# Operands of a last pass on VectorE, its products reordered, and loads moved in SyncE's queue

## The chip, the cores and the metric

The kernel runs on one core of a Trainium2 chip. The metric is the device time of one execution in microseconds, as the median of several runs. A separate execution is taken with the hardware profiler; all profile rows below are from that one execution.

## What is computed

An attention layer with a memory term feeds a mixture of four experts. All arrays are float32.

```python
# attention: B, H, S, D = 4, 8, 576, 64
scores = where(causal, -1e9, q @ k.T / sqrt(D))
a      = softmax(scores);  local = a @ v
q_p    = phi(q)                                  # phi(x) = (x if x > 0 else exp(x) - 1) + 1
mem    = (q_p @ M_prev) / (q_p @ z_prev + 1e-6)
x      = g * mem + (1 - g) * local               # g = sigmoid(beta), per head
x      = x.transpose(0, 2, 1, 3).reshape(2304, 512)
# experts: E, F = 4, 1024
p   = domain_probs / domain_probs.sum(-1)
out = sum over e of p[:, e] * (relu(x @ w1[e]) @ w2[e])
```

## The kernel before

Every operand of a large product is split into a high part (the value rounded to the fast matmul type, written by ScalarE or GpSimd) and a remainder (value minus high part, written by VectorE or GpSimd). A product is then three matmuls: high by high, high by remainder, remainder by high.

**Phases.** The experts are worked off in 37 phases; a phase is one half of one expert's 1024 hidden columns. In phases 0 to 28 one or two groups of 256 tokens are live. A phase has `mm1` (four blocks `fc` of hidden columns, each followed by a relu `hh` on ScalarE and a remainder `hl` on VectorE) and `mm2` (one product `y` per 128 tokens, scaled and added into `acc` by VectorE). The attention of tokens still to come is cut into steps, kept in a list that is sorted by slot and priority (`ev(slot, priority, function)`), and a planner interleaves these steps with the matmul parts by estimated costs. All attention steps are issued by phase 27.

**The last pass.** Phases 29 to 36 handle the last 768 tokens, six tiles of 128, for all experts. There `mm1` uses a scheme with seven block products in place of eight. The token matrix is cut into four blocks, and seven operands A11, S1, S2, A12, S3, S4, A22 are made of them once (`x_ops`, L946 to L978): plain blocks, or sums and differences of blocks. S3's difference is stored in the row buffer `trow`. They are made in pieces during phases 27 and 28, one piece ahead of every third matmul part. `put` (L956 to L959) writes a high part on ScalarE and a remainder on the engine it is given. The weights are turned into the corresponding seven operands by `wt_prep` (L980 to L1003), two sets per phase: four sums `tsum` (L992 to L995), three copies `wth` on ScalarE (L996 to L998), three remainders `wtl` (L999 to L1001). The sets of phase 29 are made in `mm2` of phase 28.

`tail_mm1` (L1005 to L1046) issues the seven products of a half phase, each six matmuls of 384 columns, into three PSUM banks X, Y, Z. Several products accumulate in one bank: A11, S2, S3, A22 in X, and S1, S4 in Y. What stands in a bank after a product is read by ScalarE (`keep`, into `trow`) or VectorE (`add`) before the next product may add to it. `done` makes the relu and the remainder. `tail_mm2` (L1048 on) makes the six products `yt`.

**Raw weights.** `w_dma` loads the next 256 KB block of weights into a ring `stg` of four buffers. `w_prep` (L224 to L243) turns a block into high part and remainder and then issues the load of the block four further on, which takes the buffer just used. All loads, the copies of k and q within SBUF (`dup_k` and the copies into `qz`, in `t_trk` and `t_trq`) and the output stores are issued from SyncE's one queue, in program order.

**Attention loads.** There are 28 tasks of four or five slots, each for two heads. `t_load` (L292) loads q, k and v of a task into one of two sets of buffers; it is issued seven slots ahead of the task's first slot `s0` (nine for the first task). The transposes of k come at `s0 - 4`, those of q at `s0 - 3`, the first operation on q at `s0 - 5`, the split of v at `s0`.

Of the kernel before, what the change touches and what calls it, by code (L numbers as in the profile page):

```python
# [10 lines left out]
AF = mybir.ActivationFunctionType  # L11
ALU = mybir.AluOpType
# [45 lines left out]
def tile_attention_moe(  # L58
# [13 lines left out]
    nc = tc.nc  # L72
# [127 lines left out]
        for fc in (range(HF) if i < PH0 else (0, 2, 1, 3))  # L200
    ]
    NSTG = 4
    wpos = {"dma": 0, "prep": 0}
    stg = {}

    def w_dma():
        j = wpos["dma"]
        if j >= len(wseq):
            return
        wpos["dma"] += 1  # L210
        i, kind, fc = wseq[j]
        e, hf = halves[i]
        f0 = (hf * HF + fc) * P
        t = sp.tile([P, DM], F32, tag="stg", name=f"stg{j}", bufs=NSTG)
        stg[j] = t
        if kind == "1":
            nc.sync.dma_start(
                out=t.rearrange("p (c f) -> p c f", c=NKD),
                in_=w1[e, :, f0 : f0 + P].rearrange("(c p) f -> p c f", p=P),
            )  # L220
        else:
            nc.sync.dma_start(out=t, in_=w2[e, f0 : f0 + P, :])

    def w_prep(i, kind, pool=False):  # L224
        last_ = PH0 - 3 <= i < PH0
        act = (kind == "1" or i < START[1] or last_) and not pool
        j = wpos["prep"]
        if j >= len(wseq) or wseq[j][0] != i or wseq[j][1] != kind:
            return
        wpos["prep"] += 1  # L230
        fc = wseq[j][2]
        t = stg.pop(j)
        hi, lo = (w1s if kind == "1" else w2s)[fc]
        if kind == "1":
            hi = hi.rearrange("p c f -> p (c f)")
            lo = lo.rearrange("p c f -> p (c f)")
        if act:
            nc.scalar.activation(hi, t, AF.Copy)  # L238
        else:
            nc.gpsimd.tensor_scalar(hi, t, 1.0, 1.0, ALU.mult, ALU.mult)  # L240
        dve = (last_ and fc % 2) or (i < START[1] and fc < PR["lod"])
        (nc.vector if dve else nc.gpsimd).tensor_tensor(lo, t, f(hi), ALU.subtract)  # L242
        w_dma()  # L243


    bdat = {}
# [42 lines left out]
    ]  # L289
    NSLOT = pos  # L290

    def t_load(t):  # L292
        for n, src, c0 in (("q", q, t.cs[0]), ("k", k, 0), ("v", v, 0)):
            nfull = min(t.nk, NCH - 1) - c0
            for j in range(2):
                s_ = src[t.b, 2 * t.a + j]
                nc.sync.dma_start(  # L297
                    out=t.nat[n][:, 0:nfull, j],
                    in_=s_[c0 * P : (c0 + nfull) * P].rearrange("(c p) d -> p c d", p=P),
                )  # L300
            if t.nk == NCH:
                for r in {"q": (D,), "k": (0,), "v": (0, D)}[n]:
                    nc.sync.dma_start(
                        out=t.nat[n][r : r + S - 4 * P, nfull],
                        in_=src[t.b, 2 * t.a : 2 * t.a + 2, 4 * P : S].rearrange(
                            "h p d -> p h d"
                        ),
                    )
# [411 lines left out]
    def ev(slot, prio, fn, cost=0.0):  # L720
        events.setdefault(slot, []).append((prio, len(events.get(slot, [])), fn, cost))
# [6 lines left out]
    for t in tasks:  # L728
        s0 = t.s0
        ld = s0 - 9 if t.i < 1 else s0 - 7  # L730
        PQ = PR
        if t.run not in seen:
            seen.add(t.run)
            ev(s0 - 9, 9, lambda r=t.run: batch_load(r))
            ev(s0 - 6, 9, lambda r=t.run: batch_prep(r))
        ev(ld, 8, lambda t=t: t_load(t))
        ev(s0 + PQ["phi1"][0], PQ["phi1"][1], lambda t=t: t_phi1(t))
        ev(s0 + PQ["phi2"][0], PQ["phi2"][1], lambda t=t: t_phi2(t))
        ev(s0 + PQ["phi3"][0], PQ["phi3"][1], lambda t=t: t_phi3(t))
        ev(s0 + PQ["trq"][0], PQ["trq"][1], lambda t=t: t_trq(t), 109.0 * len(t.cs))  # L740
        ev(s0 + PQ["trq"][0] + 1, 0.4, lambda t=t: run(t.lo_q))
        ev(s0 + PQ["trk"][0], PQ["trk"][1], lambda t=t: t_trk(t), 109.0 * t.nk)
        ev(s0 + PQ["trk"][0], 0.5, lambda t=t: run(t.lo_k))
        ev(s0, PQ["v"], lambda t=t: t_v(t))
        ev(s0 + PQ["trqp"][0], PQ["trqp"][1], lambda t=t: t_trqp(t), 109.0 * len(t.cs))
        ev(s0 + PQ["trqp"][0], 4.5, lambda t=t: run(t.lo_qp))
# [204 lines left out]
    def x_ops():  # L951

        X, s_ = tail["x"], tail["s"]
        s3 = tail["r"][:, 0:2]

        def put(n, src, eng):  # L956
            hi, lo = X[n]
            nc.scalar.activation(hi, src, AF.Copy)
            eng.tensor_tensor(lo, src, f(hi), ALU.subtract)  # L959

        def plain(n, i, k):
            return [lambda: put(n, a_blk(i, k), nc.gpsimd)]

        def summed(n, eng, dst, a, b, op):
            return [
                lambda: eng.tensor_tensor(dst, a, b, op),
                lambda: put(n, dst, eng),
            ]

        return (  # L970
            plain("A11", 0, 0)
            + summed("S1", nc.vector, s_, a_blk(1, 0), a_blk(1, 1), ALU.add)
            + summed("S2", nc.vector, s_, s_, a_blk(0, 0), ALU.subtract)
            + plain("A12", 0, 1)
            + summed("S3", nc.gpsimd, s3, a_blk(0, 0), a_blk(1, 0), ALU.subtract)
            + summed("S4", nc.vector, s_, a_blk(0, 1), s_, ALU.subtract)
            + plain("A22", 1, 1)
        )  # L978

    def wt_prep(i):  # L980

        j = wpos["prep"]
        if j >= len(wseq) or wseq[j][0] != i or wseq[j][1] != "1":
            return
        wpos["prep"] += 2
        t1, t2 = stg.pop(j), stg.pop(j + 1)
        hi, lo = tail["w"][wseq[j][2]]
        t = tail["t"]
        b11, b21, b12, b22 = t1[:, 0:GW], t1[:, GW:], t2[:, 0:GW], t2[:, GW:]
        t1 = t1.rearrange("p (n w) -> p n w", w=GW)  # L990
        gp = nc.gpsimd.tensor_tensor
        gp(t[:, 0], b12, b11, ALU.subtract)  # L992
        gp(t[:, 1], b22, t[:, 0], ALU.subtract)
        gp(t[:, 2], b22, b12, ALU.subtract)
        gp(t[:, 3], b21, t[:, 1], ALU.subtract)  # L995
        nc.scalar.activation(hi[:, 0:2], t1, AF.Copy)  # L996
        nc.scalar.activation(hi[:, 2], b22, AF.Copy)
        nc.scalar.activation(hi[:, 3:7], t, AF.Copy)  # L998
        gp(lo[:, 0:2], t1, f(hi[:, 0:2]), ALU.subtract)  # L999
        nc.vector.tensor_tensor(lo[:, 2], b22, f(hi[:, 2]), ALU.subtract)  # L1000
        nc.vector.tensor_tensor(lo[:, 3:7], t, f(hi[:, 3:7]), ALU.subtract)  # L1001
        w_dma()
        w_dma()  # L1003

    def tail_mm1(i, p):  # L1005
        wh, wl = tail["w"][p]
        r = tail["r"]
        bank = {}

        def product(x, n, b):  # L1010
            first = b not in bank
            if first:
                bank[b] = tail["ps"].tile([P, 512], F32, tag="tc", name=f"tc{i}_{p}{b}", bufs=5)
            ah, al = tail["x"][x]
            for c in range(2):
                cs = slice(c * P, (c + 1) * P)
                for z, (w_, x_) in enumerate(((wh, ah), (wh, al), (wl, ah))):
                    nc.tensor.matmul(  # L1018
                        bank[b][:, 0:TB],
                        lhsT=w_[:, n, cs],  # L1020
                        rhs=x_[:, c],
                        start=first and c == 0 and z == 0,
                        stop=c == 1 and z == 2,
                        skip_group_check=True,
                    )
            return bank[b][:, 0:TB]

        def keep(o, n):
            nc.scalar.activation(r[:, n], o, AF.Copy)

        def done(src, blk, fc):
            h_, l_ = tail["h"][blk][0][fc], tail["h"][blk][1][fc]
            nc.scalar.activation(h_, src, AF.Relu)
            nc.vector.scalar_tensor_tensor(l_, src, 0.0, f(h_), ALU.max, ALU.subtract)  # L1034

        def add(o, n, blk, fc):
            nc.vector.tensor_tensor(r[:, n], o, r[:, n], ALU.add)  # L1037
            done(r[:, n], blk, fc)

        keep(product("A11", 0, "X"), 0)  # L1040
        keep(product("S1", 3, "Y"), 1)
        keep(product("S2", 4, "X"), 2)
        add(product("A12", 1, "Z"), 0, 0, p)
        add(product("S3", 5, "X"), 1, 1, p + 2)
        add(product("S4", 2, "Y"), 2, 0, p + 2)
        done(product("A22", 6, "X"), 1, p)  # L1046

    def tail_mm2(i, tts):  # L1048
        e = halves[i][0]
# [384 lines left out]
```

## Time and profile before

| what | value |
|---|---|
| median of 3 runs | 1062.28 us (1061.09 to 1063.99) |
| profiled execution | 1065.9 us |
| its span, first to last instruction | 1064.0 us |
| mean granted TensorE clock | 0.982 |
| TensorE matmul busy | 1009.3 us, 95% of the span |
| VectorE, ScalarE, GpSimd busy | 720.0, 514.2, 613.0 us |
| mean DMA rate | 110 GB/s |

Busy shares are means over stages of different kinds: the main loop of phases 0 to 28 with attention in between, the two phases in which the last pass is prepared, and the last pass. PE is TensorE, DVE is VectorE, ACT is ScalarE, POOL is GpSimd, SP is SyncE; `L242` is line 242 of the kernel. A name such as `w2l<-stg,w2h` is the tile written and the tiles read.

### The profile page before, as it was taken

Reading aid. Unit: us, or ns where it says so; the run is one execution under the profiler, and the core shown is the slowest. Engines: PE = TensorE matmul, PEld = TensorE weight load, DVE = VectorE, ACT = ScalarE, POOL = GpSimd, SP = SyncE. Lnnn points to the kernel's source line nnn. Section 1 sums busy time; section 2 is a strip of 40 time slices with the busy share of each in tenths; the row PEclk is TensorE's granted clock in tenths of the full one; section 3 lists DMA queues with packets and bytes.
Section 4 is the critical chain, followed back from the end, with each engine's and each line's share of the span. In section 5 each row is a group of like instructions: output and inputs, shape, how many; then the busy total and the mean of one; then the engine's idle time right before and its main releaser. Section 6 shows DMA issues by size and latency. Waiting matters only on the chain.

```text
span 1064.0 us, 16442 instructions
## 1 busy us (share of the span) xinstructions
PE 1009.3 (95%) x5312; PEld 856.6 (81%) x5312; DVE 720.0 (68%) x1705; ACT 514.2 (48%) x1213; POOL 613.0 (58%) x652
## 2 busy tenths in 40 slices
PE   5799999999999999999999999999978999999998
PEld 3588778877888887878888888889867888888887
DVE  5588878887787787787787777777554444544443
ACT  4476756665555554554555454554543233333231
POOL 4668767575546555554655754657576564445540
PEclk8899999999999999999999999999988999999999
DMA  6546653454444444344445244434533222122211
GB/s 135 120 119 180 172 152 109 114 155 115 117 128 121 121 122 110 109 124 117 114 110 134 82 128 116 117 97 114 152 123 97 71 79 64 56 60 64 76 40 59
DMA packets 205956, 116.86 MB, mean 110 GB/s; under 512 B 100272, under 2 KB 181680, under 8 KB 205872
## 3 DMA queue, kind: packets, MB, share of 16 engines
q1 hardware_dynamic: 205200, 115.56, 39.5%
q8 instruction: 42, 0.69, 0.3%
q10 hardware_dynamic: 672, 0.27, 0.1%
q14 instruction: 42, 0.34, 0.1%
HBM read 100.57 MB, written 4.72 MB: 99 GB/s over the span
## 4 chain that ended last, share of the span: by engine, by line
PE 70%; DVE 13%; POOL 5%; issue 4%; ACT 4%; DMA 3%; SPq 2%; DVEq 0%; POOLq 0%; ACTq 0%
PE y L853 19%; PE h L823 17%; PE yt L1059 12%; PE o L706 3%; PE pt L343 3%; PE sp L595 3%; PE tc_1X L1018 2%; PE tc_0X L1018 2%; DMA stg<-in_moe_w_dram 2%; POOL w2l L242 2%; DVE trow L1037 2%; DVE hl L833 1%; SPq L297 1%; POOL w1l L242 1%; DVE hl L1034 1%
## 5 line engine op out<-in xcount | busy, mean ns | idle before, releaser
L242 POOL TENSOR_TENSOR w1l<-stg,w1h 128x512 fp32r<-128x512 f32 x110 | 143.9, 1313 | 162.0 <-ACT w1h L238 150.9
L242 POOL TENSOR_TENSOR w2l<-stg,w2h 128x512 fp32r<-128x512 f32 x142 | 186.4, 1315 | 16.7 <-ACT w2h L238 6.7
L823 PE MATMUL h<-xh,w1h 128*128 128x512 f32 (+1 forms) x464 | 178.4, 385 | 0.2 <-ACT w1h L238 0.2
L823 PE MATMUL h<-xh,w1l 128*128 128x512 f32 (+1 forms) x464 | 167.1, 360 | 4.2 <-POOL w1l L242 4.2
L823 PE MATMUL h<-xl,w1h 128*128 128x512 f32 (+1 forms) x464 | 166.0, 358 | 0.7 <-DVE xl L787 0.7
L853 PE MATMUL y<-w2h,hh 128*128 128x512 f32 x384 | 160.5, 418 | 0.9 <-ACT w2h L238 0.8
L853 PE MATMUL y<-w2l,hh 128*128 128x512 f32 x384 | 151.7, 395 | 2.9 <-POOL w2l L242 2.3
L853 PE MATMUL y<-w2h,hl 128*128 128x512 f32 x384 | 151.6, 395 | 0.6 <-DVE hl L833 0.6
L833 DVE SCALAR_TENSOR_TENSOR hl<-h,hh 128x512 fp32r<-128x512 f32 (+1 forms) x116 | 69.1, 596 | 77.9 <-ACT hh L832 77.2
L823 PEld LDWEIGHTS h<-xh,w1l 128*128 128x128 f32 x464 | 89.4, 193 | 17.5 <-POOL w1l L242 4.6
L832 ACT ACTIVATE hh<-h 128x512 fp32r<-128x512 f32 (+1 forms) x116 | 60.7, 523 | 81.0 <-PE h L823 80.0
L823 PEld LDWEIGHTS h<-xh,w1h 128*128 128x128 f32 x464 | 89.7, 193 | 9.7 <-ACT w1h L238 0.4
L823 PEld LDWEIGHTS h<-xl,w1h 128*128 128x128 f32 x464 | 90.0, 194 | 8.6 <-DVE xl L787 1.0
L642 ACT ACTIVATE pth<-pt 128x384 fp32r<-128x384 f32 (+3 forms) x128 | 50.5, 420 | 92.0 <-PE pt L343 90.7
L869 DVE SCALAR_TENSOR_TENSOR acc<-y,pn,acc 128x512 f32<-128x512 f32 x84 | 62.7, 747 | 43.4 <-PE y L853 43.1
L853 PEld LDWEIGHTS y<-w2h,hl 128*128 128x128 f32 x384 | 72.3, 188 | 17.1 <-DVE hl L833 1.0
L853 PEld LDWEIGHTS y<-w2l,hh 128*128 128x128 f32 x384 | 72.8, 190 | 15.0 <-POOL w2l L242 4.2
L240 POOL TENSOR_SCALAR w2h<-stg 128x512 fp32r<-128x512 f32 x120 | 78.4, 653 | 7.2 <-PE yt L1059 7.2
L853 PEld LDWEIGHTS y<-w2h,hh 128*128 128x128 f32 x384 | 72.7, 189 | 11.8 <-ACT w2h L238 1.1
L238 ACT ACTIVATE w1h<-stg 128x512 fp32r<-128x512 f32 x112 | 68.8, 625 | 6.4 <-DMA stg<-in_moe_w_dram 5.3
L1072 DVE SCALAR_TENSOR_TENSOR xt<-yt,pn,xt 128x512 f32<-128x512 f32 x42 | 31.5, 751 | 56.4 <-PE yt L1059 56.4
L343 PE MATMUL pt<-ident,s 128*128 128x128 f32 (+1 forms) x376 | 60.9, 273 | 4.6 <-DVE ptl L644 4.5
(294 smaller groups left out, 2427.9 us busy)
## 6 DMA issues: line engine op xcount, KB each, us to landing
stg<-in_moe_w_dram SPq DMA_DIRECT2D x296, 256.0 KB, 2.8
natall<-in_k_dram SPq DMA_DIRECT2D x34, 128.0 KB, 2.8
natall<-in_v_dram SPq DMA_DIRECT2D x32, 128.0 KB, 2.6
natall<-in_q_dram SPq DMA_DIRECT2D x60, 64.0 KB, 2.8
out_dram<-acc SPq DMA_DIRECT2D x12, 256.0 KB, 2.2
kha<-kha SPq DMA_DIRECT2D x16, 128.0 KB, 3.1
khb<-khb SPq DMA_DIRECT2D x16, 128.0 KB, 2.9
natall<-in_k_dram SPq DMA_DIRECT2D x28, 64.0 KB, 2.3
```

What stands on the lines that cost most here:

```text
L238: nc.scalar.activation(hi, t, AF.Copy)
L240: nc.gpsimd.tensor_scalar(hi, t, 1.0, 1.0, ALU.mult, ALU.mult)
L242: (nc.vector if dve else nc.gpsimd).tensor_tensor(lo, t, f(hi), ALU.subtract)
L343: nc.tensor.transpose(dst, src, ident[0:n, 0:n])
L642: nc.scalar.activation(dh, src, AF.Copy)
L823: nc.tensor.matmul(pt[0][:, cols], lhsT=w_[:, c], rhs=x_[:, c, cols], start=(c == 0 and z == 0), stop=(c == NKD - 1 and z == 2),)
L832: nc.scalar.activation(h_, pt[0][:, cols], AF.Relu)
L833: nc.vector.scalar_tensor_tensor(l_, pt[0][:, cols], 0.0, f(h_), ALU.max, ALU.subtract)
L853: nc.tensor.matmul(pt[0], lhsT=h_[fc][:, tk], rhs=w_, start=(fc == 0 and z == 0), stop=(fc == HF - 1 and z == 2),)
L869: nc.vector.scalar_tensor_tensor(acc[g, tt], pt[0], pe, acc[g, tt], ALU.mult, ALU.add)
L1018: nc.tensor.matmul(bank[b][:, 0:TB], lhsT=w_[:, n, cs], rhs=x_[:, c], start=first and c == 0 and z == 0, stop=c == 1 and z == 2, skip_grou ...
L1059: nc.tensor.matmul(o, lhsT=h_[fc][:, tk], rhs=w_, start=(z == 0 and fc == p and y == 0), stop=(z == 1 and fc == p + 2 and y == 2),)
```

## The change

It has three parts. In `x_ops` the remainders of A11, A12 and A22 and the difference and remainder of S3 are made on VectorE, not GpSimd, and the pieces come in another order; `wt_prep` of phase 29 makes its four sums and the remainder of the two plain blocks on VectorE. In `tail_mm1` the products come in the order A11, S1, S2, S4, S3, A12, A22, and the remainders are issued after the next addition. In the loads, the load that a preparation releases is issued at the head of the next preparation (`w_more`), and q and k of a task are loaded at `s0 - 9`, v at the old place.

```diff
     def w_prep(i, kind, pool=False):
...
+        w_more()
         wpos["prep"] += 1
...
-        w_dma()
+        wpos["due"] += 1
...
+    def w_more():
+        while wpos["due"]:
+            wpos["due"] -= 1
+            w_dma()
...
-        ev(ld, 8, lambda t=t: t_load(t))
+        ev(s0 - 9, 8, lambda t=t: t_load(t, "qk"))
+        ev(ld, 8, lambda t=t: t_load(t, "v"))
...
         def plain(n, i, k):
-            return [lambda: put(n, a_blk(i, k), nc.gpsimd)]
+            return [lambda: put(n, a_blk(i, k), nc.vector)]
...
             + summed("S2", nc.vector, s_, s_, a_blk(0, 0), ALU.subtract)
+            + summed("S4", nc.vector, s_, a_blk(0, 1), s_, ALU.subtract)
+            + summed("S3", nc.vector, s3, a_blk(0, 0), a_blk(1, 0), ALU.subtract)
             + plain("A12", 0, 1)
-            + summed("S3", nc.gpsimd, s3, a_blk(0, 0), a_blk(1, 0), ALU.subtract)
-            + summed("S4", nc.vector, s_, a_blk(0, 1), s_, ALU.subtract)
             + plain("A22", 1, 1)
...
     def wt_prep(i):
...
+        w_more()
         wpos["prep"] += 2
...
-        gp = nc.gpsimd.tensor_tensor
+        gp = (nc.vector if i == PH0 else nc.gpsimd).tensor_tensor
...
-        w_dma()
-        w_dma()
+        wpos["due"] += 2
...
-        def done(src, blk, fc):
+        def relu(src, blk, fc):
+            nc.scalar.activation(tail["h"][blk][0][fc], src, AF.Relu)
+
+        def rest(src, blk, fc):
             h_, l_ = tail["h"][blk][0][fc], tail["h"][blk][1][fc]
-            nc.scalar.activation(h_, src, AF.Relu)
             nc.vector.scalar_tensor_tensor(l_, src, 0.0, f(h_), ALU.max, ALU.subtract)

-        def add(o, n, blk, fc):
+        def add(o, n):
             nc.vector.tensor_tensor(r[:, n], o, r[:, n], ALU.add)
-            done(r[:, n], blk, fc)
+            return r[:, n]
...
         keep(product("S2", 4, "X"), 2)
-        add(product("A12", 1, "Z"), 0, 0, p)
-        add(product("S3", 5, "X"), 1, 1, p + 2)
-        add(product("S4", 2, "Y"), 2, 0, p + 2)
-        done(product("A22", 6, "X"), 1, p)
+        c12 = add(product("S4", 2, "Y"), 2)
+        relu(c12, 0, p + 2)
+        c22 = add(product("S3", 5, "X"), 1)
+        relu(c22, 1, p + 2)
+        rest(c12, 0, p + 2)
+        c11 = add(product("A12", 1, "Z"), 0)
+        relu(c11, 0, p)
+        rest(c22, 1, p + 2)
+        c21 = product("A22", 6, "X")
+        relu(c21, 1, p)
+        rest(c11, 0, p)
+        rest(c21, 1, p)
```

## Rows read from the trace of the kernel before

**Rows 1.** The page, part 1: busy us, share of the span, instructions.

```profile
PE 1009.3 (95%) x5312; PEld 856.6 (81%) x5312; DVE 720.0 (68%) x1705; ACT 514.2 (48%) x1213; POOL 613.0 (58%) x652
```

**Rows 2.** Stretches: length, busy us of PE, PEld, DVE, ACT, POOL, clock, DMA share, GB/s.

```profile
260.00:745.00 485.00, 478.17 (x2523) 401.98 (x2522) 368.70 (x922) 253.38 (x593) 279.09 (x279) 1.00 0.42 115
...
752.86:764.18 11.32, 11.32 (x74) 10.35 (x73) 5.78 (x10) 5.95 (x12) 4.54 (x4) 1.00 0.58 183
...
764.30:796.00 31.70, 26.49 (x144) 22.80 (x143) 20.95 (x26) 15.79 (x30) 25.16 (x17) 0.89 0.42 133
796.00:819.42 23.42, 18.88 (x86) 17.18 (x85) 11.31 (x16) 7.83 (x16) 16.92 (x18) 0.85 0.34 101
...
835.79:851.47 15.68, 15.17 (x86) 14.53 (x85) 6.84 (x13) 5.85 (x12) 8.05 (x9) 1.00 0.23 67
```

**Rows 3.** Chain of waits in phase 30: start us, length us, what.

```profile
838.94 1.05 PE tc_0Z L1018 x6
...
840.08 0.57 DVE trow L1037
...
840.67 0.54 ACT hh L1033
...
841.23 0.56 DVE hl L1034
841.79 0.48 DVE trow L1037
...
842.31 1.32 PE tc_0X L1018 x6
```

**Rows 4.** Waits, 819.42 to 1044 us: total us, times, longest us.

```profile
PEld tc_0X L1018 <- DVE trow L1037: 4.0, 7, 0.6
```

**Rows 5.** Timeline of phase 27: start us, length us, instruction.

```profile
769.80 0.95 DVE L959 TENSOR_TENSOR S1l<-xsum,S1h 128x768 fp32r<-128x768 f32 x1
769.92 1.97 POOL L242 TENSOR_TENSOR w2l<-stg,w2h 128x512 fp32r<-128x512 f32 x1 [0.59 <-ACT w2h L238]
770.78 1.92 DVE L966 TENSOR_TENSOR xsum<-xsum,xt 128x768 f32<-128x768 f32 x1
```

**Rows 6.** Instructions on `stg`; last row `tsum`, 790 to 820 us: ns min/median/max, starts.

```profile
L995 POOL TENSOR_TENSOR tsum<-stg,tsum x16: 717/742/1057, 794.4 to 1021.8; 128x256 f32<-128x256 f32 x16
L1000 DVE TENSOR_TENSOR wtl<-stg,wth x16: 416/551/684, 794.2 to 1023.4; 128x256 fp32r<-128x256 f32 x16
L999 POOL TENSOR_TENSOR wtl<-stg,wth x16: 1262/1298/1302, 795.3 to 1022.5; 128x512 fp32r<-128x512 f32 x16
...
L242 DVE TENSOR_TENSOR w1l<-stg,w1h x6: 680/702/1373, 751.0 to 782.7; 128x512 fp32r<-128x512 f32 x6
...
L1001 DVE TENSOR_TENSOR wtl<-tsum,wth x2: 1225/1225/1225, 796.5 to 801.8; 128x1024 fp32r<-128x1024 f32 x2
```

**Rows 7.** Groups, 764.2 to 796 us: busy us, mean ns, idle before and releaser.

```profile
L966 POOL TENSOR_TENSOR trow<-xt 128x768 f32<-128x768 f32 x1 | 1.9, 1851 | 0.0
...
L959 DVE TENSOR_TENSOR S2l<-xsum,S2h 128x768 fp32r<-128x768 f32 x1 | 1.0, 958 | 0.6 <-ACT S2h L958 0.6
...
L958 ACT ACTIVATE S3h<-trow 128x768 fp32r<-128x768 f32 x1 | 0.8, 845 | 4.6 <-POOL trow L966 4.6
```

**Rows 8.** Timeline of TensorE, first products of the last pass.

```profile
802.25 0.69 PE L1018 MATMUL tc_0X<-S2h,wth 128*128 128x384 f32 x1 [3.54 <-ACT trow L1029]
```

**Rows 9.** Waits of SyncE's queue and of ScalarE, whole span.

```profile
SPq L222 <- POOL w1l L242: 217.1, 89, 6.9
...
ACT w1h L238 <- DMA stg<-in_moe_w_dram: 5.3, 8, 1.6
```

**Rows 10.** Waits of TensorE, 45 to 150 us and 150 to 280 us.

```profile
PE tk L343 <- DMA natall<-in_k_dram: 4.6, 2, 4.1
...
PE tk L343 <- DMA natall<-in_k_dram: 2.0, 1, 2.0
```

**Rows 11.** Timeline of SyncE's queue: loads of q of the second task.

```profile
47.72 1.12 SPq L297 DMA_DIRECT2D natall<-in_q_dram  x2
```

More of the change, by code (lines that the diff above doesn't have):

```diff
@@ L202, in tile_attention_moe @@
     NSTG = 4
-    wpos = {"dma": 0, "prep": 0}
+    wpos = {"dma": 0, "prep": 0, "due": 0}
     stg = {}
@@ L290, in tile_attention_moe, with t_load @@
     NSLOT = pos
-    def t_load(t):
+    def t_load(t, names="qkv"):
         for n, src, c0 in (("q", q, t.cs[0]), ("k", k, 0), ("v", v, 0)):
+            if n not in names:
+                continue
             nfull = min(t.nk, NCH - 1) - c0
```

## The prediction

> **What bounds the kernel now.** I read the page's busy times first: TensorE works 1009.3 us of the 1064.0 us span [rows 1]. At its present matmuls and clock a change can therefore win at most its idle time, 54.7 us, and what slow-clock stretches cost.
>
> Next the table of stretches, to see where the idle time lies [rows 2]. From 260 to 745 us TensorE is idle for 6.8 us in 485, so whatever happens to loads or engines there is covered by matmuls. Two places are worse. From 764.3 to 796.0 us (phases 27 and 28, in which the operands of the last pass are made) it is idle 5.2 us, and the clock is 0.89. From 796.0 to 819.42 us (first products of the last pass) 4.5 us, clock 0.85. The same step of the next phase, 835.79 to 851.47 us, takes only 15.68 us, at a clock of 1.00.
>
> Phase 26 ran from 752.86 to 764.18 us, 11.32 us, TensorE never idle, with the same matmuls as 27 or 28 [rows 2]. Two such phases would be 22.6 us; they take 31.7. So the transition loses 9.1 us there and 23.42 - 15.68 = 7.7 us in the first products: 16.8 us in all.
>
> In the chain of waits of a later phase [rows 3] the reader is to see the one stall that is left. Products A11, S1, S2, A12, S3, S4 follow each other at 1.04 to 1.05 us. A22 adds into the bank that S3 used, so it needs the VectorE addition that reads S3. That addition stands on VectorE behind the remainder `hl` of the product before, which in turn waits for ScalarE's relu: 0.57 + 0.54 + 0.56 + 0.48 us in a row. Six matmuls of A22 then take 1.32 us instead of 1.04, and begin 0.24 us late. Sum 0.52 us, once per half phase, in all 16 halves; the waits list shows it 7 times for the first half in the seven undisturbed phases, up to 0.6 us [rows 4], and the second half has the same row.
>
> **The change, part by part.**
>
> *Operands on VectorE.* A timeline shows what VectorE and GpSimd do to each other [rows 5]: S1's remainder takes 0.95 us on VectorE; GpSimd's `w2l`, started 0.12 us later, takes 1.97 us where it otherwise takes 1.3 [rows 6]; and VectorE's next sum of the same 768 columns takes 1.92 us. The two do such operations in turn. So I add both engines' operations into one queue, by their undisturbed times. For 768 columns that is 0.96 us on VectorE (S2l) and 1.85 us on GpSimd (S3's sum, its nearest to alone) [rows 7]; for 512, 0.68 and 1.28; for 256, 0.42 and 0.74; for 1024 on VectorE 1.22 [rows 6].
>
> Before, from 764.3 us until the second set of weights is ready at 803.0 us (801.8 + 1.2, [rows 6]): GpSimd 6 remainders of weights (7.7 us), 5 operations of 768 columns (9.2), 8 sums of 256 (5.9), 2 remainders of 512 (2.6), together 25.4 us; VectorE 6 x 0.96 + 6 x 0.68 + 2 x 0.42 + 2 x 1.22 = 13.1 us. Together 38.5 us, and the stretch lasts 38.7: this queue is the bound of the transition. After: GpSimd 7.7 us; VectorE 13.1 + 5 x 0.96 + 8 x 0.42 + 2 x 0.68 = 22.6 us. Together 30.3 us, that is **8.2 us less**. VectorE itself is busy 20.95 of 31.7 us now [rows 2], part of it held up by GpSimd; with 9.5 us more it stays just within the stretch, so it is close to being the bound.
>
> That queue reaches TensorE through ScalarE, which works in order: S3h waits 4.6 us for GpSimd's sum [rows 7], and the weight copies and relus behind it are late. Then the second set of weight sums on GpSimd holds ScalarE, so that the copy of A11's product is late and S2 waits 3.54 us [rows 8]. After the change the first is gone, since S3 is summed two pieces ahead of its copy; of the second some stays, because two sets of sums and remainders on VectorE are still 4.0 us each, 4 x 0.42 + 0.68 + 0.42 + 1.22. The slow-clock stretches (0.89, 0.85) should shrink with the waits; I add nothing for that. Bounds: nothing, if VectorE's queue takes over; 16.8 us, if all loss goes. I take -8.2, nearest to the counted rows.
>
> The Trainium skill, SBUF — State Buffer, "SBUF: two separate sides", says that a VectorE operation with two SBUF inputs and a GpSimd operation that reads SBUF lock each other out for a whole instruction. By that rule only the difference of durations is won, 8.2 us; if the engines ran freely beside each other, GpSimd's 25.4 us would leave the path and up to 16.8 us could go. The trace agrees with the rule, by the 1.97 and 1.92 us above.
>
> *Products reordered.* S4 now comes ahead of S3, and its remainder is made after S3's addition. In rows 3 an addition starts 0.09 us after its product ends and takes 0.57. S3's is now the next thing on VectorE, and A12's 1.04 us stand between S3 and A22: 1.04 - 0.09 - 0.57 leaves 0.38 us, less what A22's first weight load is ahead of its matmul. So the stall goes: 16 x 0.52 = -8.3 us. What is late next: the remainder of c11 must be done before the copy of the next half's A11 overwrites that row, and S2 of that half, in the same bank, needs the copy. Counted from the start of a half by the durations of [rows 3], S4's addition runs from 4.25 to 4.82 us, S3's from 5.29 to 5.86, S4's remainder to 6.4, A12's addition to 6.97 and its relu to 7.5, S3's remainder to 7.5, c11's remainder to 8.1. The copy wants to start at 8.41 and, at 0.54 like a relu, ends at 8.95; S2 begins at 9.36. The slack is 0.31 and 0.41 us. GpSimd's sums of the next phase run there, and two of 0.74 us [rows 6] ahead of remainders would leave 1.48 - 0.72 = 0.76 us of wait, 6.1 in eight phases. I take a fifth of that, 1.3. Net -7.0, bounds -2.2 and -8.3.
>
> *Loads.* In the main loop SyncE's queue waits 217 us in total for `w1l` [rows 9], and what stands behind it is late. A raw-weight load now comes one preparation later: its four-deep ring looks three ahead. In the last pass nothing else is on that queue, so there nothing moves except that one load now follows an output store. q and k go out two slots sooner. What is won is TensorE's waits for k: 4.6 us from 45 to 150 us, of which 4.1 in one piece, and 2.0 us from 150 to 280 us [rows 10]. The first of these loads is issued at 47.72 us, behind the copies that wait for the preceding task's transposes [rows 11]; now it goes ahead of those. Counting the one piece and the 2.0 whole, that is -6.0. Against it: ScalarE waits 5.3 us in total for raw weights now [rows 9], and it relus and copies behind that. If that doubles and a third of it reaches TensorE, +2.0. Net -4.0, bounds +5.3 and -6.0. The 28 extra planned events of cost 400 shift the interleaving evenly; main-loop idle is small, so nothing.
>
> Sum: -8.2 - 7.0 - 4.0 = -19.2 us. The profiled execution took 1065.9 us, so 1046.7 with a profile; the median of the runs shown is 1062.28, 3.6 lower, so **1043 us**.
>
> **Rivals.**
>
> *The queue only moves to VectorE.* Its remainders `hl` and the accumulations stand in order behind the new sums; the 1.92 us sum [rows 5] is the sort that becomes common if GpSimd wins each turn. Against it: per operation VectorE needs little over half of GpSimd's time [rows 6, 7]. Transition 0: 1062.3 - 11.0 = 1051.
>
> *The wait goes from A22 to S2 of the next half.* For it: the slack is short, and two engines share the turns. Against it: VectorE's operations are short and GpSimd's sums come once per half. Tail -8.3 + 6.1 = -2.2: 1062.3 - 14.4 = 1048.
>
> *The weight ring starves* (the other side). Each of 28 tasks puts six loads on SyncE's queue, about 0.55 us each [rows 11], in all 3.3 us, and a raw-weight load that was ahead of them now stands behind. ScalarE waits for it in order and holds relus. At 1.0 us per task it costs 28 us: 1043 + 28 = 1071. It decides from 19.2 / 28 = 0.7 us per task on. Against it: preparations in the loop come some 3 to 4 us apart, so three ahead is about 10 us, and ScalarE waits only 8 times now, at most 1.6 us [rows 9].
>
> **How the numbers follow.** Forecast 0.50 (own range 1036 to 1048), VectorE as the new bound 0.21, wait at S2 0.16, starved ring 0.13. The last is mostly a loss (0.08), near its deciding point no change (0.05). A difference of 0.3%, 3.2 us, is about what a measurement of this kernel can tell from none. Faster 0.87, within 0.3% 0.05, slower 0.08. The range runs from 1036 (8.3 in the tail, 12 of the 16.8 in the transition, 6 at the start) to 1056 (the first two rivals together: 1062.3 - 2.2 - 4.0).
>
> **What would show it.** Stretch from the start of A11h to the first `yt` 45 to 48 us long instead of 55; S3h without its wait; later halves of products at 7.3 us each and no wait of A22 for VectorE; no 4 us gap of TensorE near 48 us. It would be wrong if `trow` copies stop S2 in every phase, if VectorE is near 100% busy in phases 27 and 28, or if `w1h <- stg` waits grow to tens of us.

## The result, and the profile after

The changed kernel takes 1045.49 us (median of 4 runs, 1044.56 to 1050.02) against 1062.72 us for the kernel before (also 4 runs, 1061.09 to 1063.99). The ratio is 0.9847, with a 95% interval of 0.9816 to 0.9879: it is faster by 17.2 us, where 19.2 were forecast. The profiled execution took 1045.51 us, its span is 1043.7 us.

The page's busy times (busy us, share of the span, instructions) answer to [rows 1]:

```profile
PE 1000.2 (96%) x5312; PEld 851.2 (82%) x5312; DVE 735.7 (70%) x1720; ACT 516.6 (49%) x1213; POOL 594.2 (57%) x637
```

TensorE's instructions are the same 5312, and its idle time fell from 54.7 to 43.5 us. Fifteen operations went from GpSimd to VectorE, and VectorE is busy 15.7 us more: more than the fifteen undisturbed durations of the prediction add (9.5 us). Where the excess comes from is shown below.

The table of stretches answers to [rows 2] (length, then busy us of PE, PEld, DVE, ACT, POOL, clock, DMA share, GB/s): phase 26, phases 27 and 28, the first products of the last pass, and the same step one phase later.

```profile
743.19:754.42 11.23, 11.23 (x74) 10.27 (x74) 5.78 (x10) 6.07 (x13) 4.71 (x4) 1.00 0.60 179
754.42:786.20 31.78, 28.09 (x156) 23.08 (x155) 30.09 (x39) 17.66 (x33) 9.48 (x7) 0.95 0.46 134
786.20:804.59 18.39, 14.79 (x74) 14.30 (x74) 11.35 (x19) 7.10 (x14) 11.55 (x12) 0.91 0.42 129
820.95:835.83 14.88, 14.86 (x85) 14.54 (x85) 7.83 (x13) 6.38 (x13) 8.11 (x9) 1.00 0.24 71
```

Three things are to be read here. The stretch of phases 27 and 28 did not become shorter (31.7 and 31.78 us), but VectorE is now busy 30.09 us of it, where it was 20.95. The first products fell from 23.42 to 18.39 us. The step of a later phase fell from 15.68 to 14.88, and TensorE is idle for 0.02 us in it.

The span is 20.3 us shorter, in three places by start times in the two traces: the making of A11h begins at 754.4 instead of 764.2 us (-9.8); from there to the first `yt` (the transition) it takes 50.2 instead of 55.2 us (-5.0); and from the first `yt` of phase 29 to that of phase 36, seven phases take 31.22 us each instead of 32.05 (-5.8; what follows is 0.3 us longer). The first of these holds an accident: the profiled execution of before took 3.2 us more than its median, and kernels with the same code up to that point start A11h anywhere from 753.6 to 757.2 us (the experiments show it).

**Later phases.** The chain of waits of the changed kernel in phase 31 (start us, length us, what) answers to [rows 3]. The first three lines are S3, A12 and A22 of the first half; then come A11, S1, S2 and S4 of the second:

```profile
856.37 1.04 PE tc_0X L1028 x6
857.41 1.04 PE tc_0Z L1028 x6
858.45 1.04 PE tc_0X L1028 x6
859.49 1.04 PE tc_1X L1028 x6
860.53 1.04 PE tc_1Y L1028 x6
861.58 0.02 issue
861.59 1.33 PE tc_1X L1028 x6
862.92 1.05 PE tc_1Y L1028 x6
```

S3, A12 and A22 follow each other at 1.04 us: the wait of A22 [rows 4] is gone. S2 of the next half now takes 1.33 us and starts 0.02 late, so 0.31 us of the 0.52 came back in another place, in one of the two halves. The timeline of the three other engines there says why (start us, length us, engine, line):

```profile
857.78 0.74 POOL L1004 TENSOR_TENSOR tsum<-stg,tsum 128x256 f32<-128x256 f32 x1
...
857.92 1.01 DVE L1046 SCALAR_TENSOR_TENSOR hl<-trow,hh 128x384 fp32r<-128x384 f32 x1
...
859.49 1.05 POOL L1006 TENSOR_TENSOR tsum<-stg,tsum 128x256 f32<-128x256 f32 x1
...
859.99 0.97 DVE L1046 SCALAR_TENSOR_TENSOR hl<-trow,hh 128x384 fp32r<-128x384 f32 x1
...
861.05 0.49 ACT L1039 ACTIVATE trow<-tc_1X 128x384 f32<-128x384 f32 x1 [0.71 <-DVE hl L1046]
```

Two remainders, of c12 and of c11, take 1.01 and 0.97 us where such a one takes 0.56 [rows 3], each beside a sum on GpSimd. The copy of A11's product waits 0.71 us for the second, and S2 waits for the copy. Of the seven phases, six take 31.24 to 31.28 us; the last, in whose products GpSimd has no sums of a next phase to make, takes 30.95.

**The transition.** TensorE's timeline has three waits of `tc` products left in the first products, answering to [rows 8]:

```profile
785.38 0.44 PE L1028 MATMUL tc_0Y<-S1h,wtl 128*128 128x384 f32 x1 [0.43 <-DVE wtl L1012]
788.98 0.45 PE L1028 MATMUL tc_0X<-S2h,wth 128*128 128x384 f32 x1 [2.61 <-ACT trow L1039]
799.12 0.44 PE L1028 MATMUL tc_1X<-S2h,wth 128*128 128x384 f32 x1 [0.99 <-ACT trow L1039]
```

S2's wait fell from 3.54 to 2.61 us only. ScalarE's timeline shows what keeps the copy: it stands behind the weight copy of the second set, which waits 2.27 us for the last sum, now on VectorE. S3h, which waited 4.6 us [rows 7], waits 0.44:

```profile
771.71 0.85 ACT L968 ACTIVATE S3h<-trow 128x768 fp32r<-128x768 f32 x1 [0.44 <-DVE trow L976]
...
787.49 1.06 ACT L1009 ACTIVATE wth<-tsum 128x1024 fp32r<-128x1024 f32 x1 [2.27 <-DVE tsum L1006]
...
788.45 0.47 ACT L1039 ACTIVATE trow<-tc_0X 128x384 f32<-128x384 f32 x1
```

**Loads.** SyncE's timeline of the changed kernel, answering to [rows 11], has q and k of the second task at 34.64 us instead of 47.72:

```profile
34.64 1.11 SPq L306 DMA_DIRECT2D natall<-in_q_dram  x2
35.79 0.98 SPq L306 DMA_DIRECT2D natall<-in_k_dram  x2
```

The waits of SyncE's queue and of ScalarE over the whole span answer to [rows 9] (total us, times, longest):

```profile
SPq L222 <- POOL w1l L249: 114.9, 54, 6.8
...
SPq L387 <- ACT kha L376: 71.0, 14, 10.7
SPq L387 <- ACT khb L376: 57.5, 19, 6.3
...
ACT w1h L245 <- DMA stg<-in_moe_w_dram: 5.3, 7, 1.7
```

The queue's wait for `w1l` halved, but it did not go away: the waits of the copies `kha` and `khb`, 30.5 us together before, are now 128.5. All waits of the queue add up to 668.2 us before and 651.6 now. ScalarE waits for raw weights 5.3 us, exactly what it was: the ring of four does not starve. TensorE's waits from 45 to 280 us hold no wait for k any more; the first entry is another one, of 4.5 us in six pieces:

```profile
PE o L548 <- DVE ptl L534: 4.5, 6, 1.5
```

### The profile page after: what moved, and what is told of

Read it like the earlier page. It is cut to its first block, busy times and chain, and to the rows that moved or that the text cites. A ratio compares the mean times of both kernels' runs of the same rounds, so it can differ in the third digit from the quotient of the medians.

```text
span 1043.7 us, 16414 instructions
## 1 busy us (share of the span) xinstructions
PE 1000.2 (96%) x5312; PEld 851.2 (82%) x5312; DVE 735.7 (70%) x1720; ACT 516.6 (49%) x1213; POOL 594.2 (57%) x637
## 4 chain that ended last, share of the span: by engine, by line
PE 77%; DVE 11%; POOL 4%; issue 3%; ACT 2%; DMA 1%; SPq 0%; ACTq 0%; POOLq 0%; DVEq 0%
PE y L863 20%; PE h L833 18%; PE yt L1079 13%; PE o L715 3%; PE sp L604 3%; PE pt L352 3%; PE tc_1X L1028 3%; PE tc_0X L1028 3%; PE tc_0Y L1028 2%; PE tc_1Y L1028 2%; POOL w1l L249 1%; DVE hl L843 1%; POOL w2l L249 1%; DMA stg<-in_moe_w_dram 1%; PE tc_1Z L1028 1%
## 5 line engine op out<-in xcount | busy, mean ns | idle before, releaser
L863 PEld LDWEIGHTS y<-w2h,hh 128*128 128x128 f32 x384 | 72.8, 190 | 11.8 <-ACT w2h L245 1.1
```

Of the source, the lines that this page charges most:

```text
L863: nc.tensor.matmul(pt[0], lhsT=h_[fc][:, tk], rhs=w_, start=(fc == 0 and z == 0), stop=(fc == HF - 1 and z == 2),)
```

## The experiments

Each kernel was compared with the kernel before on the same chip. The table has the median, its difference to the before of that chip, and three numbers of the profile: the start of A11h, the transition from there to the first `yt`, and the mean of seven later phases, all in us.

```
kernel                               median    diff   A11h   transition  phase
before                               1062.72           764.2   55.2      32.05
the change                           1045.49  -17.2    754.4   50.2      31.22
e1  both load edits alone            1058.0    -4.5    757.2   53.3      32.04
e2  early q and k alone              1057.03   -5.4    756.9   53.2      32.04
e3  reordering alone                 1055.79   -6.7    763.2   54.3      31.22
e4  operands alone                   1060.61   -1.9    761.2   50.6      32.04
e12 reordering and operands          1053.37   -8.9    761.8   50.3      31.21
e5  the change once more             1046.37  -16.4    757.2   49.9      31.21
e11 change, raw loads at old place   1047.33  -15.0    757.6   48.4      31.21
e6  change, c11's remainder earlier  1045.33  -17.4    757.0   50.1      30.96
e10 change, all sums on VectorE      1043.35  -19.0    754.1   50.2      30.95
e8  change, GpSimd idle in 26 to 28  1044.47  -18.3    754.3   48.1      31.21
e7  change, second weight set later  1042.26  -20.5    753.6   47.4      31.21
e9  change with e6, e7, e8           1038.41  -23.9    755.5   44.0      30.95
```

**e1, both load edits alone.** The kernel before with the `due` counter and the split loads of the change, nothing else:

```diff
...
+        w_more()
...
-        w_dma()
+        wpos["due"] += 1
...
-        ev(ld, 8, lambda t=t: t_load(t))
+        ev(s0 - 9, 8, lambda t=t: t_load(t, "qk"))
+        ev(ld, 8, lambda t=t: t_load(t, "v"))
```

> The kernel before with both load edits and nothing else. Theory A, the loads took away TensorE's waits for k and what follows them: phases 1 to 26 run 7 to 10 us earlier than in the kernel before, the time is 1053 to 1056 us, and the last pass is as before, 32.05 us a phase. Theory B, the earlier start in the trace of the changed kernel is the granted clock of the first 75 us (0.81 and 0.89 before, 1.00 after), which is not the kernel's doing: 1060 to 1063 us.

It took 1058.0 us, ratio 0.996 [0.9946, 0.9975]: a gain of 4.5 us, between the ranges of its two theories. The windows of the start show where it came from. First the kernel before, then e1 (the clock is the third number from the end; 1.00 is the upper of its two levels, 2.4 GHz, and 1.2 GHz the lower):

```profile
40.00:50.00 10.00, 7.88 (x51) 6.69 (x51) 4.05 (x11) 3.38 (x9) 3.44 (x8) 0.82 0.17 41
50.00:60.00 10.00, 8.06 (x38) 7.55 (x39) 4.06 (x16) 4.47 (x14) 2.45 (x4) 0.66 0.18 42
```

```profile
40.00:50.00 10.00, 9.18 (x74) 8.50 (x71) 6.05 (x19) 6.18 (x19) 7.24 (x18) 1.00 0.31 74
50.00:60.00 10.00, 9.96 (x68) 8.82 (x66) 9.61 (x26) 8.05 (x23) 5.80 (x6) 1.00 0.50 144
```

Before, TensorE runs 89 matmuls in these 20 us, with the 4.1 us wait for k from 47.9 to 51.9 [rows 10] and a granted clock of 0.66 behind it. With the loads ahead of the transposes it runs 142 matmuls at 1.00. The other profiles go the same way: in those with the old loads (e3, e4, e12) the mean clock from 40 to 60 us is 0.83, in those with early q and k it is 1.00, but for e11 with 0.92 (0.84 from 40 to 50 us, after 0.69 to 0.82 since 10 us, and 1.00 from 50 to 60 us). So behind the wait for k there is a slow stretch, and with the wait it is gone.

**e2, early q and k alone.** Only the split of `t_load`, raw weights as before:

```diff
...
-        ev(ld, 8, lambda t=t: t_load(t))
+        ev(s0 - 9, 8, lambda t=t: t_load(t, "qk"))
+        ev(ld, 8, lambda t=t: t_load(t, "v"))
```

> The kernel before with q and k loaded at s0 - 9 and nothing else; raw weights are loaded where they were. Theory A in its simple form, the waits of TensorE for k (4.1 and 2.0 us) are the whole gain of the loads: the same time as with both load edits, within 2 us, 1054 to 1057 us. Theory C, the later issue of raw weights frees SyncE's queue and wins on its own: 1058 us, some 3 us short of both edits.

1057.03 us, ratio 0.9956 [0.9939, 0.9974], as much as both together. The gain of the loads is that of q and k. The later raw weights are worth nothing that shows.

**e11, the change with raw loads at their old place.** The other half of the same question, asked of the whole change:

```diff
-        w_more()
...
-        wpos["due"] += 1
+        w_dma()
...
```

> The changed kernel with the raw weights' load issued right behind its own preparation, as before; q and k still at s0 - 9. Theory A, the early q and k are the whole gain of the loads and the later raw weights are worth nothing: 1045 to 1047 us as the change, within 2 us. Rival, the later issue keeps SyncE's queue from waiting on GpSimd and is worth something together with the rest: 1049 us or more. A third outcome, the later loads cost time near 110 us, where TensorE waits for weights: 1043 us.

1047.33 us, ratio 0.9862 [0.9843, 0.9881], against 0.9847 [0.9816, 0.9879] for the change: the intervals overlap. Its queue waits for `w1l` as long as that of before, and for the copies of k as little:

```profile
SPq L222 <- POOL w1l L248: 214.2, 88, 9.0
...
SPq L386 <- ACT khb L375: 17.3, 13, 7.5
...
SPq L386 <- ACT kha L375: 10.7, 8, 3.0
```

So the later loads took about 100 us off the wait for `w1l` and put about 100 us on the copies behind: all waits of the queue add up to 654.6 us here and 651.6 in the change. The queue did not wait less, and nothing was won.

Its transition, 48.4 us, is below that of the change (50.2 and 49.9). S2 starts as late, 34.65 us after A11h against 34.6, and after the same wait of 2.6 us. The difference lies behind it, in the granted clock of the next 5 us, first in the change, then here:

```profile
788.98:793.98 5.00, 5.00 (x20) 5.00 (x21) 1.38 (x2) 1.34 (x3) 4.51 (x5) 0.66 0.59 188
```

```profile
792.28:797.28 5.00, 5.00 (x29) 5.00 (x30) 3.30 (x5) 1.88 (x4) 4.12 (x4) 1.00 0.28 99
```

From S2 to the first `yt` it takes 13.8 us at the higher clock, 15.6 in the change. So up to 1.8 us of a transition can be the clock of that execution, and it isn't shown what decided it; what an edit does to the queue of operands is read from the start of S2.

**e3, reordering alone.** The kernel before with the new order of products, relus and remainders:

```diff
-        add(product("A12", 1, "Z"), 0, 0, p)
-        add(product("S3", 5, "X"), 1, 1, p + 2)
-        add(product("S4", 2, "Y"), 2, 0, p + 2)
-        done(product("A22", 6, "X"), 1, p)
+        c12 = add(product("S4", 2, "Y"), 2)
+        relu(c12, 0, p + 2)
...
```

> The kernel before with the new order of products and remainders alone. Theory A: no A22 wait in any half phase, but S2 of the second half waits 0.3 us: phases of 31.2 us against 32.05, 7 x 0.8 = 5.8 us less and up to 1 us more in the first phase of the pass, 1056 us. Rival, the wait moves with its full 0.52 us to S2: 32.0 us a phase and 1062 us.

1055.79 us, ratio 0.9939 [0.9919, 0.9959]. Its later phases take 31.22 us, exactly those of the change, and the transition is 0.9 us shorter: 7 x 0.83 + 0.9 = 6.7 us, which is also the difference of the medians.

**e4, operands alone.** The kernel before with the engine edits and the new order of the operands' pieces:

```diff
-            return [lambda: put(n, a_blk(i, k), nc.gpsimd)]
+            return [lambda: put(n, a_blk(i, k), nc.vector)]
...
-        gp = nc.gpsimd.tensor_tensor
+        gp = (nc.vector if i == PH0 else nc.gpsimd).tensor_tensor
```

> The kernel before with the operands on VectorE (and their new order) alone. Theory A, both engines' operations stand in one queue and it gets shorter: from A11's copy to the first yt product 55.2 us before, 50 to 52 us now, VectorE busy about 30 of the first 32 us; 1058 us. Rival, VectorE takes the queue over entirely: 55 us and 1062 us.

1060.61 us, ratio 0.9981 [0.9963, 0.9998]: 1.9 us, a good deal less than was expected of this run. The transition of its profile, 50.6 us, is that of the change. Compared with the 53.2 to 55.2 us of the four kernels with the old operands, that is 2.6 to 4.6 us less.

**e12, reordering and operands.** Both parts, without the loads.

> The kernel before with the new product order and the operands on VectorE, all loads as before. Theory A, the two parts add: 6.7 + 1.9 = 8.6 us by their times alone, 5.9 + 4.6 = 10.5 us by their stretches, 1052 to 1054 us. Rival, they help each other (the change was 3 to 4 us better than the sum of its three parts): 1050 us.

1053.37 us, ratio 0.9914 [0.9899, 0.9929]: 8.9 us, where the parts alone make 6.7 + 1.9 = 8.6. They add up.

**e5, the change once more**, on the same chip as e6, e7 and e8.

> The changed kernel itself once more, as the one that the next three are held against on the same chip. The parts alone gave 4.5, 6.7 and 1.9 us, together 13.1, the change 17.2. Theory A, the parts add and the 4 us between are the spread of the first 75 us (granted clock 0.81 to 1.00 in one and the same code): 1046 to 1049 us. Rival, the parts help each other: 1045 us again.

1046.37 us, ratio 0.9847 [0.9817, 0.9876]. The interval, 1043.3 to 1049.6 us, holds both theories, so this run does not decide between them.

**e8, GpSimd idle.** All weight remainders of phases 26 to 28 go to VectorE, so that GpSimd has nothing to do in phases 27 and 28. If the two engines get in each other's way, VectorE's six or seven extra remainders cost less than what they remove.

```diff
-        dve = (last_ and fc % 2) or (i < START[1] and fc < PR["lod"])
+        dve = last_ or (i < START[1] and fc < PR["lod"])
```

> The changed kernel with all remainders of weights in phases 26 to 28 on VectorE, so that GpSimd does nothing there. Theory A, sums of 768 columns take 1.7 to 2.05 us because they stand behind GpSimd's operations: all take 0.95 us now, and since VectorE's 0.68 replaces GpSimd's 1.3 in one queue, the transition gets 2 to 3 us shorter. Rival, those sums are slow by themselves (two operands of the same large tile): they stay at 2 us, VectorE gets 6 operations more, and the transition is 3 us longer.

1044.47 us, ratio 0.9821 [0.9791, 0.9851], which does not stand out from the change's interval. The transition is 48.1 us, shorter by about 2 us, and S2 starts 32.5 us after A11h instead of 34.6 (behind it, the clock is 0.66 for 5 us in both). One line of the kernel shows the mechanism. These are the last two of four sums for the operands of the last pass on VectorE (ns min, median, max, then start us), first in the change:

```profile
...
L976 DVE TENSOR_TENSOR xsum<-xt,xsum x1: 2039/2039/2039, 765.5 to 765.5; 128x768 f32<-128x768 f32 x1
L976 DVE TENSOR_TENSOR trow<-xt x1: 2047/2047/2047, 769.6 to 769.6; 128x768 f32<-128x768 f32 x1
```

and with GpSimd idle:

```profile
...
L976 DVE TENSOR_TENSOR xsum<-xt,xsum x1: 950/950/950, 765.0 to 765.0; 128x768 f32<-128x768 f32 x1
L976 DVE TENSOR_TENSOR trow<-xt x1: 950/950/950, 768.6 to 768.6; 128x768 f32<-128x768 f32 x1
```

The same instructions on the same data take 2.04 and 2.05 us or 0.95 us, and the difference, 1.1 us, is nearly what a remainder takes on GpSimd (1.3 us [rows 6]). This agrees with the rule of the Trainium skill, SBUF — State Buffer, "SBUF: two separate sides", that the one engine waits out a whole instruction of the other.

**e7, second weight set later.** The second set of phase 29 is made after the copy of S2's product, not in phase 28:

```diff
-                wt_prep(PH0)
+                if wseq[wpos["prep"]] == (PH0, "1", 0):
+                    wt_prep(PH0)
...
         keep(product("S2", 4, "X"), 2)
+        if i == PH0 and p == 0:
+            wt_prep(PH0)
```

> The changed kernel with the second set of weight operands of phase 29 made after the copy of S2's product in the first half, not in phase 28. Theory A, S2's wait of 2.61 us in the first phase of the last pass is the copy of A11 standing on ScalarE behind that set's copies, which wait for VectorE's sums: the wait falls under 0.5 us and the transition gets 2 us shorter, from 50.2 to 48. Rival, VectorE is the bound there, and the sums only hold S4's and S3's additions later: S2's wait goes, another of the same length comes, 50 us.

1042.26 us, ratio 0.9814 [0.9793, 0.9836]. The copy of A11's product now waits for TensorE alone, and in place of 2.61 us S2 waits for nothing. ScalarE's timeline:

```profile
783.97 0.49 ACT L1040 ACTIVATE trow<-tc_0X 128x384 f32<-128x384 f32 x1 [0.63 <-PE tc_0X L1029]
```

S2 starts at 785.46 us, 31.9 us after A11h, instead of 34.6. A wait of 1.5 us for one of VectorE's additions comes up behind it, but from S2 to the first `yt` it takes 15.5 us as in the change (15.6), because the clock is 1.00 in the 5 us behind S2, and not 0.66. So the 2.7 us stay, with that help: the transition is 47.4 us. The medians of e5 and e7 differ by 4.1 us; in the profiles, A11h alone starts 3.6 us earlier in e7, behind identical code.

**e6, c11's remainder earlier.** It is put straight behind its relu, ahead of the remainder of c22:

```diff
         relu(c11, 0, p)
+        rest(c11, 0, p)
         rest(c22, 1, p + 2)
         c21 = product("A22", 6, "X")
         relu(c21, 1, p)
-        rest(c11, 0, p)
         rest(c21, 1, p)
```

> The changed kernel with the remainder of c11 made ahead of that of c22. Theory A, the wait of 0.3 us of the second half's S2 is for the copy of A11, which waits for c11's remainder, last but one on VectorE: the wait is gone, 7 x 0.3 = 2 us less, phases of 30.95 us and not 31.25. Rival, the copy is late because ScalarE is (two relus ahead of it): no change.

The later phases take 30.96 us instead of 31.22, and TensorE has no wait of a `tc` product from 835 to 1030 us. In the median, 1045.33 us, the gain of 7 x 0.26 = 1.8 us does not stand out from the change's own interval; in the phases it does.

**e10, all weight sums on VectorE.** The rival cause for the same wait: GpSimd's sums run ahead of the remainders. The order stays as in the change:

```diff
-        gp = (nc.vector if i == PH0 else nc.gpsimd).tensor_tensor
+        gp = nc.vector.tensor_tensor
```

> The changed kernel with the four sums and the first remainder of the weight operands on VectorE in all phases of the last pass, the order of remainders as in the change. Theory A, c11's remainder is late because VectorE's remainders stand behind GpSimd's sums (about 1.0 us and not 0.56): all take 0.56 us, S2 no longer waits, phases of 30.95 us. Rival, the order alone makes the wait: 31.25 us as in the change.

1043.35 us, ratio 0.9826 [0.9808, 0.9844]; later phases 30.95 us. The same remainders that took 1.01 and 0.97 us beside GpSimd's sums, in the timeline of this kernel:

```profile
857.37 0.60 DVE L1046 SCALAR_TENSOR_TENSOR hl<-trow,hh 128x384 fp32r<-128x384 f32 x1
...
859.08 0.56 DVE L1046 SCALAR_TENSOR_TENSOR hl<-trow,hh 128x384 fp32r<-128x384 f32 x1
```

and its chain of waits, S1 and S2 of the second half:

```profile
859.98 1.04 PE tc_1Y L1028 x6
861.02 1.04 PE tc_1X L1028 x6
```

S2 takes 1.04 us. VectorE does eight sums and two remainders more in each phase, and it costs nothing: what mattered was the turns that GpSimd took.

**e9, the three together** (e6, e7 and e8), as the version that the above points to.

> The changed kernel with the three edits that each shortened it: c11's remainder earlier, the second set of phase 29's weight operands later, all remainders of weights in phases 26 to 28 on VectorE. Theory A, the three act at different places, so they add: 2.1 us in seven later phases, 2.4 to 2.8 and 1.7 to 2.1 in the transition: 50 us there become 45.5 to 46, the phases 30.95, the time 1039 to 1040 us. Rival, the two in the transition shorten the same queue on VectorE: 47 us there, 1041 to 1042 us.

1038.41 us, ratio 0.9774 [0.9758, 0.979], faster than the change and than before. The transition is 44.0 us, better than was expected. Its row in the table of stretches, and TensorE's waits of `tc` products in it:

```profile
755.50:799.54 44.04, 39.68 (x230) 34.77 (x229) 38.22 (x63) 24.77 (x47) 11.15 (x11) 1.00 0.49 154
```

```profile
PE tc_0X L1029 <- DVE trow L1050: 1.5, 1, 1.5
PE tc_0Y L1029 <- DVE wtl L1013: 0.4, 1, 0.4
```

The granted clock is 1.00 over the whole of it, where the change has 0.95 and 0.91 in its two parts. As e11 has 1.00 with the change's waits, how much of this the shorter waits did is not shown. VectorE is busy 38.22 of 44.04 us, the fullest engine after TensorE, and TensorE also waits 2.3 us for its remainders `w2l`.

## Why the prediction was right, and which step was off

The forecast was 1043 us and the time is 1045.5: the mechanisms stood, the size of one was off, and part of the closeness may be luck (see Open). By its three terms:

```
term                  predicted   alone, median [95%]        by the profile
operands on VectorE      -8.2     -1.9 [-3.9, -0.2]          -2.6 to -4.6 (transition)
products reordered       -7.0     -6.7 [-8.6, -4.4]          -6.7 (e3)
loads                    -4.0     -4.5 [-5.7, -2.7]          -7.0 (start of A11h, e1)
all                     -19.2     -17.2 [-19.6, -12.9]       -20.3 (span)
```

(The intervals are the ratios' ends times the median of before.)

**The mis-sized step** is the queue of both engines' operations for the transition, 38.5 us before and 30.3 after. Measured, from A11h to the second set of weights ready (788.58 + 1.23 = 789.81 us), the stretch is 35.4 us; before it was 38.7. So 3.3 us came off and not 8.2. Another 1.6 us of the transition's 5.0 came off behind the start of S2, where it takes 15.6 us and not 17.2; there the new order of products and a clock of 0.66, not 0.50, in the 5 us behind S2 have their share. The count left out VectorE's own work of those phases, the remainders `hl` and the accumulations, which don't belong to the change. Grouped by form on VectorE from 754.45 to 789.81 us (busy us, mean ns, idle before):

```profile
L879 DVE SCALAR_TENSOR_TENSOR acc<-y,pn,acc 128x512 f32<-128x512 f32 x5 | 3.7, 744 | 2.2 <-PE y L863 2.2
L843 DVE SCALAR_TENSOR_TENSOR hl<-h,hh 128x256 fp32r<-128x256 f32 x8 | 3.2, 412 | 0.0
```

That is 6.9 us. While GpSimd had 25.4 us of the queue, VectorE did these beside it; with VectorE at 22.6 they have to be added. And GpSimd's 7.7 us do not simply stand in the queue: six operations of 768 columns took 11.8 us in place of 6 x 0.95 = 5.7, so 6.1 us of waiting. VectorE also makes seven remainders of 512 columns in the stretch, before and after, where the prediction counted six: 0.7 us. 22.6 + 0.7 + 6.9 + 6.1 = 36.3, against 35.4 measured. That VectorE stands idle for 1.9 us and its neighbouring records overlap by 2.7 us in all nearly cancels, so the agreement is to about 1 us. VectorE had become the bound: 30.09 busy of 31.78 us in phases 27 and 28. That was the first rival, and it came true in part. It did not eat the whole gain, because per operation VectorE needs about half of GpSimd's time.

e8 and e7 bear this out from two sides. Taking away GpSimd's share saves the waiting and adds remainders of 0.68 us: the trace of e8 has seven more of them in the stretch, so -6.1 + 7 x 0.68 = -1.3 us, measured -1.7 to -2.1 against the change's two profiles. Moving one set of weights out of VectorE's queue of phase 28 took S2's wait of 2.6 us with it; measured are 2.4 to 2.8.

Two of the prediction's own signs of being wrong came up in part: VectorE is 95% busy in phases 27 and 28, and a `trow` copy stops S2 in six of the seven later phases, for 0.3 us. The transition of 45 to 48 us that it named as its sign of being right did not come: it is 50.2.

**Right: the wait of A22.** It is gone in all later phases. A half without any wait is 7 x 1.04 = 7.3 us, as forecast; one half of each phase has S2's 0.3 us on top. A phase became 0.83 us shorter, 5.8 in seven. By the prediction it would be 2 x 0.52 - 0.16 = 0.88 per phase, 6.2 in seven.

**Right in kind: the wait at S2.** The second rival came true to a small part: 0.26 us per phase (31.22 against 30.96 in e6) instead of the 0.16 taken, and far from the 0.76 of the rival. The cause is as it was put there, GpSimd's sums ahead of remainders: e10 leaves the order alone and moves the sums, e6 leaves the sums alone and moves the remainder, and each removes the whole wait.

**Right: the loads, by one half of them.** The 4.1 us wait for k is gone, and early q and k give the whole gain (e2). Of the later raw weights, neither the +2.0 us taken as a cost nor the starved ring came: ScalarE's wait for raw weights is 5.3 us as before. What the sum left out is the clock, 0.66 in the 10 us behind the wait for k. By single profiles A11h starts 7.0 us earlier in e1; by the medians the gain is 4.5 to 5.4 us, for which the waits alone (4.1 + 2.0) would do, so how much of it is clock stays undecided.

**Open.** The parts tried alone make 8.9 (e12) + 4.5 or 5.4 (e1, e2) = 13.4 to 14.3 us, the change 16.4 to 17.2. The 2 to 4 us between lie inside the intervals above, and no run tells whether they are an interaction. No term of the forecast has them: without them the time would be 1048 to 1049 us, so part of its closeness to 1043 may be luck. Where the difference lies can be narrowed: e11, which is e12 and e2 together, gives 15.0 us where these two make 14.3. Also open is what the engines and what the new order of the operands' pieces did, since e4 has both. That e4's median shows less than its transition is also not settled: the profiled execution of before is 3.2 us above its median, and the start of A11h alone differs by several us between executions.

## What to carry to other kernels

When work moves from one engine to another, add up everything that the receiving engine already does in that stretch, in order, not only the operations that the change touches; an engine that is 68% busy on the page may have no room left in the stretch that counts. Where a slow engine gets in the way of a fast one, giving the fast engine all of the work can be quicker than sharing it (e8, e10). A long wait of a DMA queue is no cost by itself, and when one falls, the others are to be added up: 100 us came off the wait for `w1l`, went onto the copies of k, and nothing was won, while one wait of 4 us that reached TensorE was worth 4 to 5. When two profiles differ in a stretch, compare the granted clock there before the code.

## What the runs showed of the hardware that was not expected

Identical code does not get the same clock at the start of the kernel. From 10 to 30 us the change has a granted clock of 1.00 in its profile:

```profile
10.00:20.00 10.00, 6.77 (x28) 3.82 (x29) 8.16 (x25) 5.13 (x17) 5.38 (x5) 1.00 0.79 176
20.00:30.00 10.00, 8.86 (x40) 5.50 (x40) 8.29 (x33) 5.57 (x20) 9.33 (x11) 1.00 0.48 117
```

and e1, whose code is the same there, ran at 0.84 and 0.65, as did the change's own repetition e5:

```profile
10.00:20.00 10.00, 6.29 (x28) 3.66 (x29) 8.09 (x25) 5.20 (x17) 5.31 (x5) 0.84 0.81 179
20.00:30.00 10.00, 8.51 (x42) 5.12 (x40) 8.69 (x35) 5.95 (x23) 9.32 (x11) 0.65 0.46 115
```

TensorE is idle for some 1 to 4 of each 10 us there. With the same code up to A11h, its start lies at 754.4 us in the change, 757.2 in its repetition and 753.6 in e7, so that a difference of 3 us between two single profiles says nothing about the code ahead of that point.
